# Sparse attention and experts on one core: the threshold of a score tile made by ACT, and the attention ordered anew

## The chip, the core and the metric

The kernel runs on one core of a Trainium2 chip. The core has engines that run side by side, each through its own instructions in order: PE (matrix products and transposes), DVE (vector work), ACT (a function of scale times input plus bias, element by element), POOL (GpSimd, vector work on SBUF), and SP, which here only issues DMAs. They wait for one another through semaphores. The metric is the device time of one execution in microseconds (us), lower is better, as the median of several runs.

## What is computed

Three steps follow each other: attention that keeps only the scores near the largest of their row, a layer of eight experts of which each token takes one, and a dense layer. The change is in the first.

```
q, k, v: [4, 8, 576, 64]; tau = 0.02
scores = (q @ k.T) / sqrt(64)
thresh = max(scores, -1) - tau
scores = where(scores >= thresh, scores, -1e9)
attn   = exp(scores - max(scores, -1))
attn   = attn / (sum(attn, -1) + 1e-9)
x      = (attn @ v) as [2304, 512]
... x goes to the expert with the largest cosine (8 experts, 512 -> 1024 -> 512)
... then 512 -> 2048 -> 512 with h * tanh(softplus(h))
```

## The kernel before

The 32 heads are handled in 16 pairs (`pair`). A pair's scores are nine tiles of 128 rows (`scores`, called for u from 0 to 8): four tiles of 576 columns for each head, and between them (u = 4) a wide one of 640 columns that holds the last 64 rows of both. Every product is made with operands split into a high and a low part, so most things come twice.

A score tile goes through five steps:

- PE makes the scores in a PSUM tile `D` (L544, or L540 and L541 for u = 4). A ring of four such tiles serves scores, transposes and PV products together.
- DVE takes the negative maximum of each row, `m` (L548).
- DVE makes the threshold `thr = -m - tau` (L549), one element per partition. `self.ntau` holds -tau.
- ACT makes `E = exp(scores + m)` (L550).
- DVE makes `P = (scores >= thr) * E` with the row sums (L551); `PL` for u = 4. The sums are read out by a second short instruction, DVE_READ_ACCUMULATOR, under the same line.

Behind that, PE transposes `P` (L569, and `PL` in L592), ACT and DVE or POOL split the transposed tile into `hi` and `lo` (ACT L573, L577, L578 and L597; DVE L574 and L598; POOL L579), PE multiplies with `V` (L614, L615), ACT copies the result `osb` out of PSUM (L618, L619), PE turns it back (L628), and DVE scales it into `xs` (L632).

A pair's queries and keys come by two loads, `raw` on the SP queue (L477) and `QK` on the POOL queue (L478), into two buffers each. POOL subtracts them (L485, L489), and ACT scales the queries by 1/8 in one instruction (L491). Only then can the pair's first scores start.

After every fourth pair a batch of eight heads is complete. Its rows `xs` are written to DRAM from the SP queue (L714), and a chain of small DVE instructions chooses the experts (`router`, L667 and on). After the third batch an early list of tokens is made for one expert (`early`, L756 to L793), so that the loads of that expert's weights (L1025) can be issued before the attention ends.

The order of the instructions on each engine is not the order of the code. A planner (`Plan.order`) keeps a list of operations with an assumed duration and a priority, and gives each engine at each step the operation that can start first by its own clock; among equals, the one with the lowest priority number. The table `PR` holds the numbers that are added to the tile's index to make these priorities (`S`, `max`, `thr`, `exp`, `stt` for the five steps above). The chip then runs each engine's list as planned, whatever the real durations are.

Of the kernel before, what the change touches and what calls it, by code (L numbers as in the profile page):

```python
# [12 lines left out]
AF = mybir.ActivationFunctionType  # L13
ALU = mybir.AluOpType
# [4 lines left out]
B, H, S, D = 4, 8, 576, 64  # L19
# [13 lines left out]
DF = 1024  # L33
FF = 2048
YW = DM + 2
PR = {'er': -2619.9, 'ep': 21.8, 'S': -1982.0, 'max': -153.5, 'nb': -889.1, 'exp': -5879.6, 'stt': -152.4, 'T': 7.7, 'Tp': 1782.0, 'p32': 220.7, 'hi': 779.9, 'lo': -419.6, 'dlo': -3008.1, 'pv0': 15.6, 'pv1': 20.3, 'po': 1302.8, 'osb': 1044.0, 'x': -0.4, 'px': 1519.1, 'xev': 285.6, 'q': -2270.7, 'scale': -1169.5, 'thr': -538.6, 'kl': -64.4, 'v': 3680.0, 'load': -688.7, 'dve_lo': (1, 4, 7), 'TL': 8.5, 'TLp': 1148.1, 'TLh': 593.3, 'TLl': -956.3, 'route': 1062.7, 'rkpos': 7.0, 'kl_dve': 0, 'q_pool': 2, 'of': 31.7, 'rd': -735.6, 'A_pool': (), 'nA': 0, 'n0': 2, 'ne': 375.2, 'ns': 340.5, 'nr': 2, 'np': -247.6}
PR2 = {'pipe': (), 'dve_hi': (0, 5, 6), 'xo': 28.3, 'ps': (9.4, 19.4), 'cd': 1400000.0, 'split': (("ACT", "DVE"), ("ACT", "POOL"), ("ACT", "DVE"), ("ACT", "DVE"), ("ACT", "DVE"), ("ACT", "POOL"), ("ACT", "DVE"), ("ACT", "DVE")), 'sl': 28000, 'll': 2000, 'pool_lo': (0, 2, 5, 7), 'gbuf': 4, 'lag': 792.0, 'fw': 807.0, 'fw_act': (1, 3), 'fw_pool': (1, 2, 3), 'n0': 0, 'n1': 0.85, 'np': 425.2, 'ld': -417.9, 'w0': -43.3, 'w1': -231.3, 'wlo': 312.9, 'xg': -217.3, 'xt': -648.5, 'xh': -515.6, 'h': -564.9, 'hs': -795.5, 'ht': -410.1, 'hh': -461.8, 'yy': -44.9, 'ye': 19.4, 'yi': 872.9, 'fy': 331.1, 'ft': 295.4, 'fx': 270.0, 'f1': -825.7, 'sg': -67.6, 'rc': 536.7, 'gg': 80.4, 'gh': -47.7, 'gl': -79.7, 'ob': -955.1, 'pt': -803.4}


# [3 lines left out]
def t_mm(m, n):  # L43
    return max(110, n / 2.4 + 14)


def t_act(n, psum=True, ptr=0):
    return (n + (61 if psum else 112)) / 1.2 + 93 * ptr


def t_dve(n, fast=False):
    return ((n / 2 if fast else n) + 65) / 0.96


def t_pool(n):
    return 2.25 * n + 100
# [26 lines left out]
class Plan:  # L83
# [8 lines left out]
    def add(self, eng, dur, fn, r=(), w=(), prio=0.0, lat=0, after=(), dma=0):  # L92
        i = len(self.ops)
        deps = set(after)
        for k in r:
            if k in self.last_w:
                deps.add(self.last_w[k])
            self.readers.setdefault(k, []).append(i)
        for k in w:
            if k in self.last_w:  # L100
                deps.add(self.last_w[k])
            deps.update(x for x in self.readers.get(k, ()) if x != i)
            self.last_w[k] = i
            self.readers[k] = []
        deps.discard(i)
        hs = []
        for k in list(r) + list(w):
            h = k[0] if isinstance(k, tuple) else k
            if isinstance(h, Handle) and h not in hs:
                hs.append(h)  # L110
                self.users.setdefault(h.group, []).append(i)
                if h.after is not None:
                    deps.add(h.after)
        self.ops.append([eng, dur, fn, deps, hs, prio, lat, dma, self.phase])
        return i
# [125 lines left out]
class Kernel:  # L241
# [34 lines left out]
    def h(self, pool, tag, shape, dt, bufs, at):  # L276
        key = (pool, tag)
        if key not in self.rings:
            self.rings[key] = Ring(bufs)
        return Handle(self.rings[key], lambda: self.pools[pool][0].tile(shape, dt, tag=tag, name=tag, bufs=bufs), at, pool, self.hooks.get(pool))  # L280
# [178 lines left out]
    def pair(self, p):  # L459
# [7 lines left out]
        qk, v = self.io["qk"][p], self.io["v"][p]  # L467
        pr = t0 + PR["load"]
        if p == 0:
# [10 lines left out]
        for j in range(2):  # L480
            pj = t0 + 4.5 * j
            first = p == 0 and j == 0
            on_dve = j < PR["kl_dve"]
            qe, qd = (nc.gpsimd, t_pool(S)) if j < PR["q_pool"] and not first else (nc.vector, t_dve(S))
            x = add("POOL" if qe is nc.gpsimd else "DVE", qd, lambda j=j, qe=qe: qe.tensor_tensor(QK()[64:128, j, 0:S], raw()[64:128, j], QK()[64:128, j, 0:S].bitcast(F32), op=ALU.subtract), r=[(raw, j)], w=[(QK, 1 + j)], prio=pj + PR["q"])  # L485
            if first:
                self.behind = [x]
            ke = nc.vector if on_dve else nc.gpsimd
            add("DVE" if on_dve else "POOL", t_dve(S) + 300 if on_dve else t_pool(S), lambda j=j, ke=ke: ke.tensor_tensor(KL()[:, j], raw()[:, 2 + j], QK()[:, 2 + j, 0:S].bitcast(F32), op=ALU.subtract), r=[(raw, j), (QK, 4 + j)], w=[(KL, j)], prio=pj + PR["kl"])  # L489

        add("ACT", t_act(2 * S, False), lambda: nc.scalar.mul(QK()[:, 0:2, 0:S], QK()[:, 0:2, 0:S].bitcast(F32), 0.125), w=[(QK, 1), (QK, 2)], prio=t0 + PR["scale"])  # L491
        add("SP", 600, lambda: nc.sync.dma_start(vraw(), v), w=[vraw], prio=pr + 9, lat=2000, dma=328e3, after=self.behind)
# [23 lines left out]
    def scores(self, p, u, QK, KL, Ps, PL, den, dk, denL):  # L516
        nc, add, h = self.nc, self.pl.add, self.h
        at = 9 * p + u
        sc = self.two(at)
        m = h("a_late", "m", [128, 1], F32, 6, at)  # L520
        thr = h("a_late", "thr", [128, 1], F32, 6, at)
        E = h("a_early", "E", [128, 640], F32, 3, at)
        if u == 4:
            js, i = (0, 1), None
            cols, w_ = (512, 576), 320
            outs, w = (lambda: PL()[:, :], lambda: denL()[:, 0:1]), [PL, denL]
        else:
            j, i = (0, u) if u < 4 else (1, u - 5)
            js = (j,)
            cols, w_ = (i * 128 + j * (QW + 64),), HD  # L530
            outs, w = (lambda: Ps[i]()[:, j * S:(j + 1) * S], lambda: den[:, j, i:i + 1]), [(Ps[i], j), (dk[j], i)]

        def mm():
            Qf = QK().rearrange("p a b -> p (a b)")
            for n in range(2):
                if u == 4:

                    for a, (k, jj, k0, o0) in enumerate(((320, 0, 0, 0), (256, 1, 0, 64)) if n == 0 else ((320, 1, 256, 0), (256, 0, 320, 0))):
                        for b, K in enumerate((QK()[:, 2 + jj, k0:k0 + k], KL()[:, jj, k0:k0 + k])):
                            nc.tensor.matmul(sc()[:, n, o0:o0 + k], lhsT=Qf[:, cols[jj]:cols[jj] + 128], rhs=K, start=(a == 0 and b == 0), stop=False)  # L540
                    nc.tensor.matmul(sc()[:, n, 256 * n:256 * n + 64], lhsT=self.corner[:, 64 * n:64 * n + 128], rhs=self.never, start=False, stop=True)  # L541
                    continue
                for a, K in enumerate((QK()[:, 2 + j, n * HD:(n + 1) * HD], KL()[:, j, n * HD:(n + 1) * HD])):
                    nc.tensor.matmul(sc()[:, n, :HD], lhsT=Qf[:, cols[0]:cols[0] + 128], rhs=K, start=(a == 0), stop=(a == 1))  # L544

        sv, Ev = (lambda: sc()[:, :, :w_]), (lambda: E()[:, 0:2 * w_].rearrange("p (a b) -> p a b", a=2))
        add("PE", 4 * t_mm(128, HD) if u != 4 else 4 * t_mm(128, 320) + 4 * t_mm(128, 256) + 220, mm, r=[(QK, x + j) for x in (1, 4) for j in js] + ([(QK, 3)] if u == 4 else []) + [(KL, j) for j in js], w=[sc], prio=at + PR["S"])
        add("DVE", t_dve(2 * w_), lambda: nc.vector.tensor_reduce(m(), sv(), axis=AX.XY, op=ALU.max, negate=True), r=[sc], w=[m], prio=at + PR["max"])  # L548
        add("DVE", 131, lambda: nc.vector.tensor_scalar(thr(), m(), -1.0, self.ntau, op0=ALU.mult, op1=ALU.add), r=[m], w=[thr], prio=at + PR["thr"])  # L549
        add("ACT", t_act(2 * w_, ptr=1), lambda: nc.scalar.activation(Ev(), sv(), AF.Exp, bias=m(), scale=1.0), r=[sc, m], w=[E], prio=at + PR["exp"])  # L550
        add("DVE", t_dve(2 * w_) + 65, lambda: nc.vector.scalar_tensor_tensor(outs[0]().rearrange("p (a b) -> p a b", a=2), sv(), thr(), Ev(), op0=ALU.is_ge, op1=ALU.mult, accum_out=outs[1]()), r=[sc, thr, E], w=w, prio=at + PR["stt"])  # L551

# [907 lines left out]
```

## Time and profile before

| | |
|---|---|
| median of 3 runs | 1101.08 us (1101.04 to 1101.51) |
| the profiled execution | 1099.78 us, its span 1098.0 us |
| attention, first to last score tile | 14 to 365 us of the span |
| its drain, and the choice of experts | 365 to 402 us |
| experts, then the dense layer | 402 us to the end |

The profile is of one execution. The span is the time from its first to its last instruction; the execution's own time is 1.8 us longer. "Busy" is time in which an engine runs an instruction. Instructions of one engine overlap a little, so a step from the start of one to the start of the next tells more of what it costs than its duration. What ends an idle stretch is called its releaser.

### The profile page before, as it was taken

The numbers are of one execution on the slowest core, as the hardware profiler recorded it, in microseconds if no ns is written. First come the engines' busy times: TensorE is split into PE (matmuls) and PEld (weight loads), VectorE is DVE, ScalarE is ACT, GpSimd is POOL, SyncE is SP. The second block draws the span as 40 slices with busy tenths as digits, with TensorE's granted clock in tenths as the row PEclk, the third lists the DMA queues.
The fourth block names the chain that finished last, engine by engine and source line by source line (L and its number), as shares of the span: only waits on it lengthen the run. The fifth ranks groups of instructions, "written<-read, shape, count | busy, mean of one in ns | idle before, by whom it ended". The sixth has DMA issues, their size and how long they took to land. (4 is left out here: it accounts for less than half of the span.)

```text
span 1098.0 us, 17382 instructions
## 1 busy us (share of the span) xinstructions
PE 1003.5 (91%) x6397; PEld 911.0 (83%) x6397; DVE 838.6 (76%) x1318; ACT 625.3 (57%) x1077; POOL 519.6 (47%) x495
## 2 busy tenths in 40 slices
PE   3899879979989969999999986999999999999997
PEld 3788778868888858979999975899999899998986
DVE  6899879978999676846678794997867768677580
ACT  4688768867877635534555543555445354453540
POOL 7688667857866523323342263633322333323322
PEclk9899899998999969999999997999999999999999
DMA  9844965694593299967679866000010100100001
GB/s 293 247 123 125 140 165 155 139 126 122 180 110 63 101 105 350 320 218 267 252 264 330 319 208 214 21 20 20 20 40 10 30 21 20 39 11 10 21 1 38
DMA packets 84700, 144.32 MB, mean 131 GB/s; under 512 B 47936, under 2 KB 47936, under 8 KB 78592
## 3 DMA queue, kind: packets, MB, share of 16 engines
q1 hardware_dynamic: 51392, 105.23, 34.6%
q0 software_dynamic: 33216, 37.93, 13.6%
q8 instruction: 51, 0.84, 0.3%
q14 instruction: 41, 0.34, 0.1%
HBM read 116.07 MB, written 27.06 MB: 130 GB/s over the span
## 5 line engine op out<-in xcount | busy, mean ns | idle before, releaser
L1322 DVE RECIPROCAL b<-p 128x512 f32<-128x512 f32 x72 | 239.3, 3339 | 19.7 <-ACT p L1319 18.2
L1325 POOL TENSOR_TENSOR lo<-c,hi 128x512 fp32r<-128x512 f32 x72 | 93.4, 1304 | 138.8 <-ACT hi L1324 127.5
L579 POOL TENSOR_TENSOR lo<-p,hi 128x512 fp32r<-128x512 f32 x96 | 122.7, 1286 | 59.4 <-ACT hi L578 51.7
L548 DVE TENSOR_REDUCE m<-D 128x1 f32<-128x576 f32 x144 | 107.5, 755 | 19.7 <-PE D L544 18.5
L550 ACT ACTIVATE E<-D,m 128x576 f32<-128x576 f32 x144 | 104.6, 751 | 21.5 <-DVE m L548 20.9
L1317 ACT ACTIVATE p<-S 128x512 f32<-128x512 f32 x72 | 43.0, 597 | 125.3 <-PE S L1304 115.3
L544 PE MATMUL D<-QK 128*128 128x288 f32 x256 | 85.3, 348 | 22.6 <-ACT QK L491 11.3
L551 DVE SCALAR_TENSOR_TENSOR P<-D,thr,E 128x576 f32<-128x576 f32 x128 | 101.9, 810 | 0.7 <-ACT E L550 0.4
L1323 DVE SCALAR_TENSOR_TENSOR c<-b,S 128x512 f32<-128x512 f32 x72 | 46.1, 656 | 71.6 <-POOL lo L1325 71.6
L569 PE MATMUL D<-ident,P 128*128 128x128 f32 x576 | 84.0, 283 | 13.1 <-DVE P L551 10.9
L991 DVE TENSOR_TENSOR wl<-raw,wh 128x1024 fp32r<-128x1024 f32 x48 | 63.3, 1339 | 36.3 <-ACT wh L989 29.7
L1082 PE MATMUL S<-xh,wh 128*128 128x256 f32 (+1 forms) x288 | 88.6, 307 | 0.0
L1082 PE MATMUL S<-xh,wl 128*128 128x256 f32 (+1 forms) x288 | 87.9, 305 | 0.1
L1082 PE MATMUL S<-xl,wh 128*128 128x256 f32 (+1 forms) x288 | 87.7, 304 | 0.0
L1304 PE MATMUL S<-hi,wh 128*128 128x256 f32 x288 | 82.3, 286 | 2.3 <-DVE c L1323 2.2
L614 PE MATMUL D<-hi,V 128*128 128x512 f32 x160 | 74.1, 463 | 10.3 <-DVE PL L551 9.4
L1304 PE MATMUL S<-lo,wh 128*128 128x256 f32 x288 | 82.2, 285 | 0.0
L1304 PE MATMUL S<-hi,wl 128*128 128x256 f32 x288 | 82.1, 285 | 0.0
L1324 ACT CAST hi<-c 128x512 fp32r<-128x512 f32 x72 | 43.9, 618 | 65.9 <-PE B L1332 52.1
L569 PEld LDWEIGHTS D<-ident,P 128*128 128x128 f32 x576 | 66.6, 148 | 16.6 <-issue 11.7
L991 POOL TENSOR_TENSOR wl<-raw,wh 128x1024 fp32r<-128x1024 f32 x16 | 40.1, 2505 | 79.4 <-ACT wh L989 79.4
L544 PEld LDWEIGHTS D<-QK 128*128 128x128 f32 x256 | 52.0, 203 | 28.6 <-ACT QK L491 11.3
(262 smaller groups left out, 3172.0 us busy)
## 6 DMA issues: line engine op xcount, KB each, us to landing
raw<-in_wm_dram SPq DMA_DIRECT2D x32, 1024.0 KB, 7.5
raw<-in_qk_dram SPq DMA_DIRECT2D x15, 1152.0 KB, 5.2
QK<-in_qk_dram POOLq DMA_DIRECT2D x15, 1152.0 KB, 8.6
fraw<-in_w_in_dram SPq DMA_DIRECT2D x16, 512.0 KB, 5.9
fraw<-in_w_out_dram SPq DMA_DIRECT2D x16, 512.0 KB, 6.7
y_dram<-osb SPq DMA_DIRECT2D x21, 257.0 KB, 5.3
vraw<-in_v_dram SPq DMA_DIRECT2D x16, 320.0 KB, 5.8
V<-in_v_dram POOLq DMA_DIRECT2D x16, 320.0 KB, 4.0
```

Source lines behind the costliest of these rows:

```text
L544: nc.tensor.matmul(sc()[:, n, :HD], lhsT=Qf[:, cols[0]:cols[0] + 128], rhs=K, start=(a == 0), stop=(a == 1))
L548: add("DVE", t_dve(2 * w_), lambda: nc.vector.tensor_reduce(m(), sv(), axis=AX.XY, op=ALU.max, negate=True), r=[sc], w=[m], prio=at + PR[" ...
L550: add("ACT", t_act(2 * w_, ptr=1), lambda: nc.scalar.activation(Ev(), sv(), AF.Exp, bias=m(), scale=1.0), r=[sc, m], w=[E], prio=at + PR[" ...
L551: add("DVE", t_dve(2 * w_) + 65, lambda: nc.vector.scalar_tensor_tensor(outs[0]().rearrange("p (a b) -> p a b", a=2), sv(), thr(), Ev(), o ...
L569: pd(nc.tensor.transpose(pt()[:, i * 128:(i + 1) * 128], Ps[i]()[:, c * 128:(c + 1) * 128], self.ident))
L579: add("POOL", t_pool(512), lambda: nc.gpsimd.tensor_tensor(lo(), p32(), hi().bitcast(F32), op=ALU.subtract), r=[p32, hi], w=[lo], prio=at ...
L614: nc.tensor.matmul(o(), lhsT=w, rhs=T[c][b](), start=(a == 0 and b == 0), stop=(a == 4 and b == 1))
L991: add(le, d, lambda: e.tensor_tensor(lo()[:, s], raw()[:, s], hi()[:, s].bitcast(F32), op=ALU.subtract), r=[kr, kh], w=[kl], prio=prio + .5)
L1082: hd(nc.tensor.matmul(hp().rearrange("p (k n) -> p k n", n=128), lhsT=a()[:, kc, f], rhs=x()[:, k0:k0 + n, kc * 128:(kc + 1) * 128], start ...
L1304: hd(nc.tensor.matmul(hp()[:, f * 256:(f + 1) * 256], lhsT=w, rhs=x, start=(n == 0), stop=(n == 11)))
L1322: add("DVE", 3270, lambda q_=q_, r_=r_: v.reciprocal(r_(), g2(q_)), r=[q_], w=[r_], prio=au + R["rc"])
L1325: add("POOL", t_pool(512), lambda gg=gg, gh=gh, gl=gl: g.tensor_tensor(g2(gl), gg(), g2(gh).bitcast(F32), op=ALU.subtract), r=[gg, gh], w= ...
```

## The change

The threshold moves from DVE to ACT: the same value, made by an activation with the identity function, scale -1 and the bias `ntau`, instead of a multiply and an add. The planner is told of 130 ns on ACT instead of 131 on DVE. And most numbers of the table `PR` are set anew, so that the planner orders the whole attention differently on all engines. `PR2`, which orders the experts and the dense layer, is as it was, and behind the dispatch every engine's order is unchanged.

```
-PR = {..., 'S': -1982.0, 'max': -153.5, 'exp': -5879.6, 'stt': -152.4, ..., 'thr': -538.6, ..., 'load': -688.7, 'TL': 8.5, ...}
+PR = {..., 'S': -2172.6, 'max': -56.7, 'exp': -3405.4, 'stt': -0.3, ..., 'thr': -14.3, ..., 'load': -124.9, 'TL': 13.9, ...}
...
-        add("DVE", 131, lambda: nc.vector.tensor_scalar(thr(), m(), -1.0, self.ntau, op0=ALU.mult, op1=ALU.add), r=[m], w=[thr], prio=at + PR["thr"])
+        add("ACT", 130, lambda: nc.scalar.activation(thr(), m(), AF.Identity, scale=-1.0, bias=self.ntau), r=[m], w=[thr], prio=at + PR["thr"])
```

What this does to the order is seen at two places. The first is DVE in the middle of the attention, behind the row sums' reciprocal of one pair. `m` is a maximum, `thr` a threshold, `P` and `PL` the products with `E`, `lo` a low part, `xs` the scaled output. Before:

```order
L548 TENSOR_REDUCE m<-D 128x1 x2
L549 TENSOR_SCALAR thr<-m,ntau 128x1 x2
L548 TENSOR_REDUCE m<-D 128x1
L551 SCALAR_TENSOR_TENSOR P,den_85<-D,thr,E 128x576
L549 TENSOR_SCALAR thr<-m,ntau 128x1
L551 SCALAR_TENSOR_TENSOR P,den_85<-D,thr,E 128x576 x2
L574 TENSOR_TENSOR lo<-D,hi 128x512
L548 TENSOR_REDUCE m<-D 128x1
L549 TENSOR_SCALAR thr<-m,ntau 128x1
L548 TENSOR_REDUCE m<-D 128x1
L551 SCALAR_TENSOR_TENSOR P,den_85<-D,thr,E 128x576
```

And in the changed kernel, from the same place:

```order
L548 TENSOR_REDUCE m<-D 128x1 x2
L551 SCALAR_TENSOR_TENSOR P,den_85<-D,thr,E 128x576 x2
L548 TENSOR_REDUCE m<-D 128x1
L574 TENSOR_TENSOR lo<-D,hi 128x512
L548 TENSOR_REDUCE m<-D 128x1
L551 SCALAR_TENSOR_TENSOR P,den_85<-D,thr,E 128x576
L632 TENSOR_TENSOR xs<-D,rd 128x5x72
L551 SCALAR_TENSOR_TENSOR PL,denL<-D,thr,E 128x640
```

The thresholds are gone, and what stood between a maximum and its product has become less: here one product, or a subtraction and a maximum.

The second is ACT while the second batch is being written to DRAM. `E` is an exponential (128x640 is the wide tile u = 4), `p` and `hi` are parts of a transposed tile, `TL` that of the wide tile, `rt` the router's. L491 is the scaling that waits for the next pair's load. Before:

```order
L726 ACTIVATE rt<-rt 128x40
L577 COPY p_4412<-D 128x512
L550 ACTIVATE E<-D,m 128x576
L578 CAST hi<-p_4412 128x512
L491 ACTIVATE QK<-QK 128x2x576
L550 ACTIVATE E<-D,m 128x640
L577 COPY p_4482<-D 128x512
L578 CAST hi<-p_4482 128x512
```

And in the changed kernel, around the same L491:

```order
L550 ACTIVATE E<-D,m 128x576
L549 ACTIVATE thr<-m,ntau 128x1
L597 CAST TL<-D 128x10x64
L550 ACTIVATE E<-D,m 128x640
L491 ACTIVATE QK<-QK 128x2x576
L549 ACTIVATE thr<-m,ntau 128x1
L577 COPY p_4472<-D 128x512
L578 CAST hi<-p_4472 128x512
```

The wide tile's exponential has moved ahead of L491, and its threshold stands behind it.

## Rows read from the trace of the kernel before

**Rows 1.** The page: the span, and the busy time of every engine with its instructions.

```profile
span 1098.0 us, 17382 instructions
...
PE 1003.5 (91%) x6397; PEld 911.0 (83%) x6397; DVE 838.6 (76%) x1318; ACT 625.3 (57%) x1077; POOL 519.6 (47%) x495
```

**Rows 2.** Windows: us, then busy us (instructions) of PE, PEld, DVE, ACT, POOL; PEclk, DMA share, GB/s.

```profile
14.00:365.00 351.00, 307.29 (x2097) 280.05 (x2097) 315.82 (x773) 270.80 (x490) 255.96 (x235) 0.95 0.69 146
...
122.00:150.00 28.00, 23.77 (x157) 21.92 (x156) 25.58 (x66) 19.66 (x41) 14.07 (x13) 0.88 1.14 139
...
216.00:243.00 27.00, 22.66 (x152) 20.29 (x151) 24.96 (x65) 19.26 (x40) 13.63 (x12) 0.94 1.15 144
...
311.00:336.00 25.00, 20.79 (x138) 18.79 (x136) 23.18 (x59) 17.62 (x38) 14.55 (x13) 0.93 1.12 109
```

**Rows 3.** Windows of 23 us, columns as above; the last row is L548 alone (DVE).

```profile
83.00:106.00 23.00, 22.02 (x156) 20.10 (x155) 21.45 (x55) 20.02 (x36) 19.69 (x18) 1.00 0.47 132
...
336.00:359.00 23.00, 21.07 (x153) 19.05 (x153) 22.38 (x53) 19.66 (x35) 17.50 (x15) 1.00 0.30 44
...
83.00:106.00 23.00, 8.12 (x11) 1.00 0.47 132
```

**Rows 4.** Timeline of DVE: start us, us, engine, instruction, count, idle time before and releaser.

```profile
209.07 0.76 DVE L548 TENSOR_REDUCE m<-D 128x1 f32<-128x576 f32 x1
209.74 0.81 DVE L551 SCALAR_TENSOR_TENSOR P<-D,thr,E 128x576 f32<-128x576 f32 x1
...
210.48 0.21 DVE L549 TENSOR_SCALAR thr<-m,ntau 128x1 f32<-128x1 f32 x1
210.60 0.81 DVE L551 SCALAR_TENSOR_TENSOR P<-D,thr,E 128x576 f32<-128x576 f32 x1
...
212.50 0.69 DVE L574 TENSOR_TENSOR lo<-D,hi 128x512 fp32r<-128x512 f32 x1 [0.34 <-ACT hi L573]
213.10 0.75 DVE L548 TENSOR_REDUCE m<-D 128x1 f32<-128x576 f32 x1
213.89 0.21 DVE L549 TENSOR_SCALAR thr<-m,ntau 128x1 f32<-128x1 f32 x1
214.02 0.81 DVE L548 TENSOR_REDUCE m<-D 128x1 f32<-128x640 f32 x1
```

**Rows 5.** Timeline of ACT, the same microseconds and columns.

```profile
208.78 2.00 ACT L550 ACTIVATE E<-D,m 128x576 f32<-128x576 f32 x3
...
211.80 0.59 ACT L573 CAST hi<-D 128x512 fp32r<-128x512 f32 x1
212.28 0.61 ACT L577 COPY p<-D 128x512 f32<-128x512 f32 x1
212.75 0.30 ACT L619 COPY osb<-D 128x128 f32<-128x128 f32 x1
212.92 0.65 ACT L578 CAST hi<-p 128x512 fp32r<-128x512 f32 x1
213.88 0.74 ACT L550 ACTIVATE E<-D,m 128x576 f32<-128x576 f32 x1 [0.32 <-DVE m L548]
```

**Rows 6.** Timeline of SP, POOL, ACT and DVE around the first batch that is complete.

```profile
122.56 1.00 SPq L714 DMA_DIRECT2D x_dram<-xs  x2
...
149.96 2.77 POOL L485 TENSOR_TENSOR QK<-raw,QK 64x576 fp32r<-64x576 f32 x2 [6.32 <-issue]
...
152.76 1.16 ACT L491 ACTIVATE QK<-QK 128x1152 fp32r<-128x1152 f32 x1 [4.80 <-POOL QK L485]
...
154.64 0.88 DVE L551 SCALAR_TENSOR_TENSOR PL<-D,thr,E 128x640 f32<-128x640 f32 x1 [4.77 <-ACT E L550]
```

**Rows 7.** Timeline of SP and PE behind the last score tile.

```profile
373.58 1.11 SPq L1025 DMA_DIRECT2D raw<-in_wm_dram  x2
...
376.50 0.52 PE L786 MATMUL D<-M,A 128*128 128x4 bf16 x15 [2.18 <-DVE M L779]
```

More of the change, by code (lines that the diff above doesn't have):

```diff
@@ L35 @@
 YW = DM + 2
-PR = {'er': -2619.9, 'ep': 21.8, 'S': -1982.0, 'max': -153.5, 'nb': -889.1, 'exp': -5879.6, 'stt': -152.4, 'T': 7.7, 'Tp': 1782.0, 'p32': 220.7, 'hi': 779.9, 'lo': -419.6, 'dlo': -3008.1, 'pv0': 15.6, 'pv1': 20.3, 'po': 1302.8, 'osb': 1044.0, 'x': -0.4, 'px': 1519.1, 'xev': 285.6, 'q': -2270.7, 'scale': -1169.5, 'thr': -538.6, 'kl': -64.4, 'v': 3680.0, 'load': -688.7, 'dve_lo': (1, 4, 7), 'TL': 8.5, 'TLp': 1148.1, 'TLh': 593.3, 'TLl': -956.3, 'route': 1062.7, 'rkpos': 7.0, 'kl_dve': 0, 'q_pool': 2, 'of': 31.7, 'rd': -735.6, 'A_pool': (), 'nA': 0, 'n0': 2, 'ne': 375.2, 'ns': 340.5, 'nr': 2, 'np': -247.6}
+PR = {'er': -3405.1, 'ep': 17.4, 'S': -2172.6, 'max': -56.7, 'nb': -889.1, 'exp': -3405.4, 'stt': -0.3, 'T': 7.9, 'Tp': 1979.4, 'p32': 1109.3, 'hi': 1626.2, 'lo': -141.9, 'dlo': -3206.2, 'pv0': 14.5, 'pv1': 20.7, 'po': 71.2, 'osb': 1407.1, 'x': -0.3, 'px': 3492.6, 'xev': 910.6, 'q': -1369.2, 'scale': -542.9, 'thr': -14.3, 'kl': -46.6, 'v': 3922.5, 'load': -124.9, 'dve_lo': (1, 4, 7), 'TL': 13.9, 'TLp': 1176.9, 'TLh': 1078.9, 'TLl': -1498.9, 'route': 2313.3, 'rkpos': 8.6, 'kl_dve': 0, 'q_pool': 2, 'of': 31.7, 'rd': -65.1, 'A_pool': (), 'nA': 0, 'n0': 2, 'ne': 375.2, 'ns': 340.5, 'nr': 2, 'np': -247.6}
 PR2 = {'pipe': (), 'dve_hi': (0, 5, 6), 'xo': 28.3, 'ps': (9.4, 19.4), 'cd': 1400000.0, 'split': (("ACT", "DVE"), ("ACT", "POOL"), ("ACT", "DVE"), ("ACT", "DVE"), ("ACT", "DVE"), ("ACT", "POOL"), ("ACT", "DVE"), ("ACT", "DVE")), 'sl': 28000, 'll': 2000, 'pool_lo': (0, 2, 5, 7), 'gbuf': 4, 'lag': 792.0, 'fw': 807.0, 'fw_act': (1, 3), 'fw_pool': (1, 2, 3), 'n0': 0, 'n1': 0.85, 'np': 425.2, 'ld': -417.9, 'w0': -43.3, 'w1': -231.3, 'wlo': 312.9, 'xg': -217.3, 'xt': -648.5, 'xh': -515.6, 'h': -564.9, 'hs': -795.5, 'ht': -410.1, 'hh': -461.8, 'yy': -44.9, 'ye': 19.4, 'yi': 872.9, 'fy': 331.1, 'ft': 295.4, 'fx': 270.0, 'f1': -825.7, 'sg': -67.6, 'rc': 536.7, 'gg': 80.4, 'gh': -47.7, 'gl': -79.7, 'ob': -955.1, 'pt': -803.4}
```

## The prediction, made before the changed kernel had run

> **What bounds the kernel now.** I read the page first [rows 1]: a span of 1098.0 us, DVE busy for 76% of it and ACT for 57%. Those shares mix four stages, so they say little. The diff changes the attention's score tiles and the numbers that order the attention; on every engine the order behind the dispatch is the same in both kernels. So I read the attention alone, from its first score tile to its last (14 to 365 us), with the view of windows [rows 2]: DVE is busy for 315.8 of these 351 us (90%), PE for 307.3, ACT for 270.8.
>
> Then I looked for what is not compute. Each time a batch of heads is complete, its rows are written to DRAM from the SP queue, and the loads of the pair after next come behind them. The timeline around the first of these [rows 6] shows the writes from 122.6 us, GpSimd idle for 6.3 us until the next QK has landed (149.96), ACT idle for 4.8 us at the scaling of that QK, L491, and DVE idle for 4.8 us, because the exponential that it waits for is queued on ACT behind L491. Three stretches of 28, 27 and 25 us have a DMA share above 1.1 [rows 2]. They end with a transfer; faster compute buys nothing in them. That leaves 351 - 80 = 271 us in which compute sets the pace.
>
> In an undisturbed stretch of those, 83 to 106 us [rows 3], DVE is busy for 21.45 of 23 us (93.3%), ACT for 20.02 (87%), and 11 tile maxima start. At 336 to 359 us DVE reaches 22.38 (97.3%): the highest share that I saw one of these two hold in such a window. So DVE sets the pace there, and ACT is only 1.4 us a window behind it. That is the number to keep in mind.
>
> **What leaves DVE.** 144 instructions of L549. Each lasts 0.21 us, but instructions overlap, so I take steps from start to start [rows 4]. A maximum followed by something independent is one step of 0.67 us (209.07 to 209.74). Followed by its own threshold it takes 0.79 (213.10 to 213.89) and the threshold another 0.13, so 0.25 us are saved. A threshold that stands elsewhere costs 0.12 (210.48 to 210.60). In the order before, 40 of the 144 stand right behind their own maximum and 104 don't: 40 x 0.25 + 104 x 0.12 = 22.5 us, 0.156 a tile. If all of it passed through in the stretches bound by compute, it would be 22.5 x 271 / 351 = 17.4 us. In the window of 23 us DVE would fall to 21.45 - 11 x 0.156 = 19.7 us.
>
> **What comes to ACT.** 144 activations of one element with a bias from memory; no row shows that form. Bounds from steps on ACT [rows 5]: the copy L619 of 128 elements takes a step of 0.17 us (212.75 to 212.92), a cast of 512 one of 0.48 (211.80 to 212.28), so 0.0008 us an element and about 0.07 for one element without the pointer. Three exponentials take 2.00 us, so a step of (2.00 - 0.74) / 2 = 0.63; less 575 x 0.0008 that leaves 0.17. The exponential too has a pointer for its bias, so it is the nearest row, and I take 0.17: 24.5 us in all, with 0.07 as the low end and 0.26 (a whole duration of such an instruction, nothing overlapped: 0.74 - 0.48) as the high one. In the window ACT goes to 20.02 + 11 x 0.17 = 21.9 us of 23: **ACT becomes the busiest engine**, and the window cannot go below that.
>
> The Trainium skill, page "ScalarE: Activation LUTs", section "What ACT_TABLE_LOAD costs", gives such an activation with a pointer about 280 ns plus 0.833 ns an element, with about 93 ns of overlap; an estimate from that page is 0.19 us a step and 27 us in all, which would make ACT's window 22.1 us. No run here shows it yet.
>
> **The new wait.** The last DVE step of a tile (L551) now needs two results of ACT. By the rows: a maximum ends at 213.85, its exponential starts at 213.88 [rows 5] and the threshold would start 0.63 us behind it, last 0.26 and be seen by DVE about 0.11 us later (the gap from the cast that ends at 212.39 to L574 at 212.50 [rows 4]): 214.88, where the exponential alone would be seen at 214.73. So each tile's chain is 0.15 us longer. One instruction in between keeps DVE busy until about 0.6 us behind the maximum, against 1.03 needed: a wait of about 0.4 us. In the changed order 33 of 144 tiles have just one instruction in between, the others two or more, so at most about 14 us of waits. They fit into the room that DVE gains (2.8 us in each of some 12 windows: 33 us), so I don't add them; they are why DVE won't set the pace any more, and if the cover is gone they cost up to 14 us.
>
> The order shows something else: at two of the three DMA stretches a threshold stands on ACT right **behind L491**, the instruction that waits for the late QK. At the second, the exponential of the wide tile moves ahead of L491, which would free it from that wait, but its threshold stays behind. So L551 of that tile waits as long as now, about 4.8 us [rows 6], and the PV products with it. The stalls stay; I count neither gain nor loss.
>
> **What is moved.** TL's transposes come five score tiles later, and V's products begin a tile earlier or later; the same instructions on the same engines, nothing added, and for PE there is cover in the 351 - 307.3 us of idle time. The loads keep their places on POOL to within one instruction of 1.3 us, and SP keeps the pattern of writes, then loads. After the last score tile the drain has another mix of transposes and products, with the same wait for the early list; what that wait is worth is 2.2 us [rows 7], so up to 2 us either way, and I take zero. The first loads of the experts' weights are issued at 373.6 us [rows 7], right behind the early choice of an expert, so they come as much earlier as the attention does: I expect what the attention gains to pass through to the end.
>
> **The sum.** ACT, at 21.9 us of work in the window and the 97.3% that DVE reaches, makes the window 22.5 us: 0.5 us of 23, 2.2%, of 271 us 5.9. No gain in 80 us, none in the drain. The profiled execution took 1099.8 us (span 1098.0), 1.3 under the median of 1101.1, so 1093.8 in such a profile, and **1095 us** as a median.
>
> **Rivals.**
> 1. DVE's whole saving arrives: ACT's step is nearer to 0.07 (window work 20.8 us), and DVE's waits fall between its own instructions. For it: ACT is idle for a quarter of the attention. Against it: the nearest row says 0.17. Up to 17.4 us: 1084.
> 2. Slower, by ACT as the new pace: everything on ACT is in order, and it also feeds POOL and the transposes, so it may not be kept as busy as DVE can be. The point that decides is a share of 95.2% (21.9 of 23). At DVE's usual 93.3% the window becomes 23.5 us: 0.5 us longer, 2.0% of 271 us, +5.5: 1107. With 0.26 a step ACT has 22.9 us to do in the window, and it is slower at any share that a row shows. For it: ACT's idle time today is mostly waiting for PE and DVE, which doesn't vanish. The Trainium skill states the same choice as a rule (page "ScalarE: Activation LUTs", section "Rules for kernel authors"): multiply and add belong on VectorE, not ScalarE. It reasons by cost per element, and no run here shows it for one element.
> 3. No change: saving and new waits cancel. The DMA stretches end when they end, and in between PE, DVE and ACT are all within 10% of each other, so each waits a little for the others: within 2.2 us of 1101.
>
> **How the numbers follow.** 0.2% of this time is 2.2 us, about what a measurement can tell from no change. Forecast (3 to 10 us less) 0.45; the whole saving (over 10 us less) 0.15; no change 0.19; slower 0.21. Faster takes the first two and a little of the third: 0.62; same 0.17; slower 0.21. The range runs from rival 1's 1084 to 1106, just short of rival 2's price. The forecast's own range is 1091 to 1098.
>
> **What would show it.** Right: L549 on ACT with a step near 0.17 us and 144 of them; ACT's busy share in an undisturbed 23 us above 93% and DVE's near 86%; the maxima 2% closer together; L491 still waiting 4 to 5 us at three places, with L551 behind it. Wrong: DVE still above 93% and the attention 15 us shorter (rival 1), or L551 waiting for L549 at far more than 33 tiles with ACT below 95% (rival 2). I would be most wrong if the moved transposes and products let PE run denser, or tear gaps that the order doesn't show: the granted clock is below full in the stalls (0.88 at 122 to 150 us [rows 2]), and more of them would cost PE twice.

## The result and the profile after

The changed kernel took 1118.1 us as the median of four executions, before 1101.3 us beside it on the same chip. One of the four (2965.84 us) is left out of the ratio; the others are 1115.14, 1115.88 and 1120.32, so that the middle one is 1115.88, 14.6 us above before. The profile is of the 1120.32. The ratio is **1.0125, 95% interval 1.009 to 1.0161**: slower by 1.25%, outside the predicted range, on the side to which I had given 0.21.

The page of the changed kernel, with the lines that answer to [rows 1]:

```profile
span 1118.3 us, 17273 instructions
...
PE 1009.2 (90%) x6397; PEld 914.5 (82%) x6397; DVE 826.9 (74%) x1174; ACT 649.2 (58%) x1221; POOL 521.8 (47%) x495
```

144 instructions have gone from DVE to ACT: DVE is busy for 11.7 us less, ACT for 23.9 more. Yet PE's busy time, for which no instruction was added, rose by 5.7 us. The windows answer to [rows 2, 3]: the attention to the end of its last score tile, the same 23 us as before, and the maxima (L548) in them. Columns as in [rows 2]: length, then busy us of PE, PEld, DVE, ACT, POOL.

```profile
14.00:379.30 365.30, 312.29 (x2094) 282.31 (x2093) 305.58 (x629) 293.98 (x631) 255.86 (x237) 0.94 0.67 141
83.00:106.00 23.00, 21.29 (x150) 18.84 (x148) 19.15 (x42) 20.97 (x43) 19.04 (x17) 1.00 0.41 123
...
83.00:106.00 23.00, 7.56 (x10) 1.00 0.41 123
```

The attention ends at 379.3 us; before it ended at 364.6. DVE is down to 83% of the undisturbed window (the prediction had about 86), ACT is at 91% (above 93), and in the same 23 us ten maxima start, not eleven. Neither engine is at a limit there, and the kernel is slower.

The view of one line, for the new activation: durations in ns (least, median, most), and who waited for it, in us and times.

```profile
L549 ACT ACTIVATE thr<-m,ntau x144: 279/293/342, 14.4 to 380.9; 128x1 f32<-128x1 f32 x144
...
  DVE P L551: 13.8, 31
  DVE PL L551: 6.8, 4
```

L551 waits for the threshold 31 + 4 times, 20.6 us in all. I first took that for the cause. The runs below show that it isn't.

**Where the time went.** Two timelines show one of the places. First ACT, around 172 us:

```profile
171.10 0.58 ACT L577 COPY p<-D 128x512 f32<-128x512 f32 x1 [0.53 <-PE D L569]
171.58 0.75 ACT L550 ACTIVATE E<-D,m 128x576 f32<-128x576 f32 x1
172.21 0.29 ACT L549 ACTIVATE thr<-m,ntau 128x1 f32<-128x1 f32 x1
172.40 0.58 ACT L577 COPY p<-D 128x512 f32<-128x512 f32 x1
```

Then PE at the same time:

```profile
169.88 0.30 PE L544 MATMUL D<-QK 128*128 128x288 f32 x1
170.01 0.29 PE L544 MATMUL D<-KL,QK 128*128 128x288 f32 x1
170.35 1.09 PE L569 MATMUL D<-ident,P 128*128 128x128 f32 x8
173.04 0.40 PE L544 MATMUL D<-QK 128*128 128x288 f32 x1 [1.59 <-ACT p L577]
...
173.91 0.44 PE L544 MATMUL D<-QK 128*128 128x288 f32 x1
174.15 0.44 PE L544 MATMUL D<-KL,QK 128*128 128x288 f32 x1
...
174.87 0.63 PE L614 MATMUL D<-hi,V 128*128 128x512 f32 x1
...
176.85 0.45 PE L614 MATMUL D<-hi,V 128*128 128x512 f32 x1
```

And the window behind the wait (PEclk is the column after the five engines):

```profile
173.00:177.00 4.00, 3.96 (x15) 3.58 (x16) 2.19 (x6) 1.92 (x5) 2.00 (x2) 0.57 0.25 83
```

PE transposes two blocks at 170.35 into one slot of D, whose ring has four. The next score tile needs a free slot, and the one that comes free is the transposed one, once both copies L577 have read it. The second copy stands on ACT behind an exponential and its threshold: it runs from 172.40 to 172.98, and PE starts at 173.04, after 1.59 us idle. That is not all. Before the wait a score matmul came every 0.13 us (169.88, 170.01); behind it they come every 0.24 (173.91, 174.15), and the granted clock from 173 to 177 is 0.57 of full, a mixture of 2.4 and 1.2 GHz. How much this pair lost is seen on DVE, from one product of a wide tile to the next, in the changed kernel and then before:

```profile
160.09 0.88 DVE L551 SCALAR_TENSOR_TENSOR PL<-D,thr,E 128x640 f32<-128x640 f32 x1
...
184.13 0.89 DVE L551 SCALAR_TENSOR_TENSOR PL<-D,thr,E 128x640 f32<-128x640 f32 x1 [0.27 <-ACT thr L549]
```

```profile
154.64 0.88 DVE L551 SCALAR_TENSOR_TENSOR PL<-D,thr,E 128x640 f32<-128x640 f32 x1 [4.77 <-ACT E L550]
...
176.11 0.87 DVE L551 SCALAR_TENSOR_TENSOR PL<-D,thr,E 128x640 f32<-128x640 f32 x1
```

That is 24.0 us for 21.5. The rest of the loss is spread: the fourth pair's PL comes 4.0 us later than before, the eighth's 8.0, the last one's 14.2.

Over the attention the view of waits has 45 waits of PE with 52.5 us in the changed kernel, 43 with 43.5 us before, and PE's busy time is 312.3 us for 306.9. These are the 14.7 us: 9.0 more of waiting, 5.4 more for the same matmuls. Of the 5.4 the clock explains about 2: by the granted clock in the trace PE is busy at 1.2 GHz for 35.0 us of the attention, before for 31.0, and what takes twice as long there loses half of the difference (an estimate). The rest comes at full clock, and no run shows why.

Nor is the wait shown above the kind that grew: for L577's copies PE (L544) waits 5.6 us in all, before 7.3. New are six waits for the low part of TL (L598), 10.8 us. The two long ones stand where the first batch is written to DRAM:

```profile
131.81 0.33 PE L615 MATMUL D<-TL,V 128*128 128x128 f32 x1 [4.59 <-DVE TL L598]
...
159.57 0.79 PE L614 MATMUL D<-hi,V 128*128 128x512 f32 x1 [5.25 <-DVE TL L598]
```

On DVE the first of these low parts stands behind the small instructions that choose the experts (L667 to L672):

```profile
129.93 1.09 DVE L672 SCALAR_TENSOR_TENSOR oh<-rt 128x40 f32<-128x40 f32 x1
130.94 0.81 DVE L598 TENSOR_TENSOR TL<-D,TL 128x640 fp32r<-128x640 f32 x1
```

The second waits for TL's first copy (L597), which stands on ACT behind L491 and so behind the late QK. Before, PE waited 3.67 and 4.75 us in that stretch, for P behind the same small instructions and for PL behind L491. So both places cost PE a wait in either kernel; in the changed one it comes by way of TL, whose move the prediction had put at no cost, and is 1.4 us longer in all.

### The profile page after: what moved, and what is told of

The parts are those of the page before. It is cut to its first block, busy times and chain, and to the rows that moved or that the text cites. A ratio compares the mean times of both kernels' runs of the same rounds, so it can differ in the third digit from the quotient of the medians.

```text
span 1118.3 us, 17273 instructions
## 1 busy us (share of the span) xinstructions
PE 1009.2 (90%) x6397; PEld 914.5 (82%) x6397; DVE 826.9 (74%) x1174; ACT 649.2 (58%) x1221; POOL 521.8 (47%) x495
## 5 line engine op out<-in xcount | busy, mean ns | idle before, releaser
L548 DVE TENSOR_REDUCE m<-D 128x1 f32<-128x576 f32 x144 | 107.1, 755 | 29.8 <-PE D L544 27.0
L550 ACT ACTIVATE E<-D,m 128x576 f32<-128x576 f32 x144 | 106.9, 754 | 31.0 <-DVE m L548 30.0
L544 PE MATMUL D<-QK 128*128 128x288 f32 x256 | 87.3, 355 | 31.8 <-ACT QK L491 11.6
L551 DVE SCALAR_TENSOR_TENSOR P<-D,thr,E 128x576 f32<-128x576 f32 x128 | 102.4, 812 | 14.4 <-ACT thr L549 13.8
L569 PE MATMUL D<-ident,P 128*128 128x128 f32 x576 | 87.3, 290 | 13.6 <-DVE P L551 5.4
L1323 DVE SCALAR_TENSOR_TENSOR c<-b,S 128x512 f32<-128x512 f32 x72 | 46.1, 656 | 71.6 <-POOL lo L1325 71.6
L991 DVE TENSOR_TENSOR wl<-raw,wh 128x1024 fp32r<-128x1024 f32 x48 | 61.6, 1303 | 38.6 <-ACT wh L989 30.9
L569 PEld LDWEIGHTS D<-ident,P 128*128 128x128 f32 x576 | 69.3, 149 | 18.9 <-issue 11.8
L544 PEld LDWEIGHTS D<-QK 128*128 128x128 f32 x256 | 52.4, 205 | 37.9 <-ACT QK L491 11.6
```

Source lines behind the costliest of these rows:

```text
L569: pd(nc.tensor.transpose(pt()[:, i * 128:(i + 1) * 128], Ps[i]()[:, c * 128:(c + 1) * 128], self.ident))
L991: add(le, d, lambda: e.tensor_tensor(lo()[:, s], raw()[:, s], hi()[:, s].bitcast(F32), op=ALU.subtract), r=[kr, kh], w=[kl], prio=prio + .5)
```

## Experiments

Two theories were set against each other at first: A, the engine (thresholds on ACT make ACT, or L551's wait for them, the pace), and B, the order (the new sequence on every engine makes PE wait). A program that emits on one engine what the planner placed on another separates them. The ratio is always to the kernel before on the same chip, and "attention" is the stretch from 14 us to the end of the last score tile of the profiled execution (before: 350.6 us).

**e4_old_lists_act: before's order on every engine; only the threshold is issued on ACT.**

```diff
-add("DVE", 131, lambda: nc.vector.tensor_scalar(thr(), m(), -1.0, self.ntau, ...
+add("DVE", 131, lambda: nc.scalar.activation(thr(), m(), AF.Identity, scale=-1.0, bias=self.ntau), ...
```

> The order of before on every engine, with only the 144 thresholds issued on ACT at their planned places. Theory A (the engine: a threshold on ACT lengthens each tile's chain, and L551 waits for it): slower than before by most of the 14 us, 1108 to 1116. Theory B (the new order of the attention costs it): within 4 us of before, 1097 to 1105, with L551 waiting for L549 under 8 us in all.

Measured: 1100.77 us, 0.9971 [0.9942, 1.0]. The windows of the attention and of two undisturbed pairs, and behind them those of before:

```profile
14.00:362.90 348.90, 310.61 (x2094) 281.19 (x2094) 299.07 (x629) 296.17 (x631) 255.83 (x238) 0.95 0.70 147
71.80:111.60 39.80, 38.68 (x275) 34.89 (x274) 35.01 (x73) 37.25 (x79) 33.24 (x28) 1.00 0.54 153
```

```profile
73.30:113.20 39.90, 37.92 (x274) 34.84 (x274) 36.93 (x92) 34.02 (x61) 33.27 (x28) 1.00 0.54 154
14.00:364.60 350.60, 306.89 (x2094) 279.65 (x2093) 315.42 (x772) 270.40 (x489) 255.56 (x235) 0.95 0.69 146
```

Two pairs last 39.8 us for 39.9, though DVE has 1.9 us less to do and ACT 3.2 more. One part of the expectation missed: L551's wait for the threshold is not under 8 us but nearly what it is in the changed kernel, and the attention is no longer for it. From the view of L551, us and times:

```profile
  ACT thr L549: 17.5, 19
```

**e5_old_lists_act_again** is the same kernel, measured more often.

> The same kernel as e4_old_lists_act (before's order on every engine, the threshold merely issued on ACT), in more rounds, since 0.9971 with an interval up to 1.0 leaves open whether the move gains anything. If PE sets the pace, the move gives only what shorter waits of PE give (37.5 us for 43.5 in its profile): 0.996 to 1.0. If DVE's relief counts, 0.98 to 0.99.

Measured: 1103.91 us, 1.0008 [0.9982, 1.0034]; attention 351.2 us. Together with e4 the move by itself makes no difference that these runs can tell. The profiles of e4 and e5, of one and the same kernel, have attentions of 348.9 and 351.2 us: a difference of 2 to 3 us between two profiles says nothing.

**e3_new_lists_dve: the changed kernel's order on every engine; the threshold is issued on DVE.**

```diff
-add("ACT", 130, lambda: nc.scalar.activation(thr(), m(), AF.Identity, ...
+add("ACT", 130, lambda: nc.vector.tensor_scalar(thr(), m(), -1.0, self.ntau, ...
```

> The changed order on every engine, with only the thresholds issued on DVE at their planned places. Theory A: back to 1098 to 1104. Theory B: stays slow, 1111 to 1120, with DVE's waits for score tiles above 18 us and L551's wait for ACT gone.

Measured: 1122.7 us, 1.0153 [1.0109, 1.0197]. Its attention, and PE's wait at the place shown above:

```profile
14.00:386.40 372.40, 318.84 (x2094) 287.64 (x2093) 322.50 (x772) 271.85 (x489) 256.72 (x237) 0.92 0.66 138
...
174.90 0.40 PE L544 MATMUL D<-QK 128*128 128x288 f32 x1 [1.41 <-ACT p L577]
175.13 0.29 PE L544 MATMUL D<-KL,QK 128*128 128x288 f32 x1
175.26 0.29 PE L544 MATMUL D<-QK 128*128 128x288 f32 x1
```

With no threshold on ACT the wait for the slot is still there, 1.41 us, 0.18 shorter: about the step of a threshold on ACT (0.19, from 172.21 to 172.40). Behind it the matmuls come every 0.13 us: here the wait was not followed by a slower clock, as it was in the changed kernel. L551's wait for ACT is down to 1.3 us, and the kernel is as slow. With e4 and e5 this makes four cases, two orders by two engines, and only the order matters: A has fallen, B holds, and the loss comes with the order.

**e1_engine_only** keeps the old table of priorities and gives the planner the threshold on ACT; **e2_table_only** takes the new table and leaves the threshold on DVE.

```diff
 e1, against before:
-add("DVE", 131, lambda: nc.vector.tensor_scalar(thr(), ...
+add("ACT", 130, lambda: nc.scalar.activation(thr(), ...
 e2, against before:
-PR = {'er': -2619.9, 'ep': 21.8, ...
+PR = {'er': -3405.1, 'ep': 17.4, ...
```

> The old table of priorities, the threshold planned and issued on ACT, so that the planner orders anew by the old numbers. Theory A: slower than before by 8 us or more. Theory B: this order is new as well, so anything from 1095 to 1112; if under 1101, the move itself can gain and the table took it away.

> The new table, the threshold planned and issued on DVE. Theory A: within 5 us of before. Theory B: slow, 1108 to 1120, as the table is made for another load of the engines.

Measured: e1 1133.58 us, 1.0272 [1.023, 1.0313]; e2 1104.99 us, 1.0012 [0.9989, 1.0034]. Both are outside what B had foreseen and within what A had, so by themselves they would have misled. But in both the planner made another order, as e3 and e4 did not, so they don't test the engine. The new table alone costs nothing; the old table with the engine changed in the plan costs more than the whole change. Priorities are read by a planner that takes, on each engine, what it thinks is ready first, so a changed engine makes it choose anew everywhere. e1's attention, and two undisturbed pairs:

```profile
14.00:388.60 374.60, 315.62 (x2096) 280.85 (x2094) 296.47 (x630) 296.20 (x631) 255.24 (x238) 0.95 0.66 137
77.70:121.00 43.30, 38.64 (x275) 34.91 (x274) 34.84 (x73) 37.24 (x79) 33.16 (x28) 1.00 0.50 140
```

The clock is full, PE has the same 38.6 us of work as in e4, and the two pairs take 43.3 us. What is added are short waits of PE, none over 1.1 us there; in the whole attention it has 72 waits with 58.8 us.

**f4_old_table_150: before, with only the planner's number for DVE's threshold at 150 in place of 131.** Every instruction and its engine stay.

```diff
-add("DVE", 131, lambda: nc.vector.tensor_scalar(thr(), ...
+add("DVE", 150, lambda: nc.vector.tensor_scalar(thr(), ...
```

> The kernel before in every operation and engine; only the planner's number for the threshold on DVE is 150 in place of 131, so the planner sets another order from the same table. If what costs in the changed kernel is that a new plan leaves an order in which PE, the pace, waited little, this shows it without a threshold on ACT and without new priorities: slower than before, ratio 1.003 to 1.015, with PE's waits in the attention above before's 43.5 us. If the order matters only through the new priorities or through ACT's queue, it is within 0.2% of before.

Measured: 1117.67 us, **1.0142 [1.0115, 1.017]**. One number that runs nowhere on the chip costs as much as the whole change. Its windows (the attention, two undisturbed pairs, 6 us of a later stretch), and a row of PE's timeline ahead of these 6 us:

```profile
14.00:384.00 370.00, 322.12 (x2095) 294.96 (x2093) 311.46 (x772) 270.90 (x489) 255.20 (x237) 0.90 0.67 139
75.50:115.40 39.90, 37.93 (x274) 34.88 (x274) 36.93 (x92) 34.02 (x61) 33.26 (x28) 1.00 0.54 154
...
258.00:261.00 3.00, 3.00 (x14) 3.00 (x14) 2.55 (x7) 1.57 (x3) 2.98 (x3) 0.50 0.43 114
261.00:264.00 3.00, 3.00 (x11) 2.61 (x11) 1.73 (x5) 0.00 (x0) 0.00 (x0) 0.50 0.94 385
...
254.52 1.94 PE L569 MATMUL D<-ident,P 128*128 128x128 f32 x8 [3.66 <-DVE lo L574]
```

The undisturbed pairs are those of before to a few hundredths. Most of the loss lies in the stretches in which a batch is written to DRAM, as at this place: PE waits 3.66 us, runs at a granted clock of 0.50 (1.2 GHz) behind the wait, and is busy for 100% of 258 to 264 us at half speed, while DVE falls to 1.73 of 3 us and ACT to nothing. In the attention PE waits 4 us longer than before and is busy 15 us longer, for the same matmuls. Here the clock explains it: PE is busy at 1.2 GHz for 61.2 us, before for 31.0, and half of the difference is the 15.

**h1_hi_back: the changed kernel with one priority set back.**

```diff
-'hi': 1626.2
+'hi': 779.9
```

> The changed kernel with one number of its table set back, that of the second copy of a transposed tile on ACT (L578, hi, from 1626.2 to the old 779.9), so that these copies stand earlier among ACT's operations. If the 14.7 us that the attention lost lie in single places of the order where PE waits for a copy or for what is made from it (two waits of L614 for lo, 4.3 and 2.9 us, and those that follow), part of it comes back: attention 356 to 362 us for 365.3, ratio 1.003 to 1.01. If the loss lies in ACT's load with the threshold, no order of the copies helps: ratio 1.01 to 1.016.

Measured: 1110.33 us, 1.0083 [1.0056, 1.0109].

```profile
14.00:372.60 358.60, 311.82 (x2094) 283.30 (x2094) 304.52 (x629) 294.31 (x631) 255.39 (x238) 0.94 0.68 143
```

The attention is 358.6 us: 6.7 of the 14.7 us come back, with ACT's load as it was. That isn't the worth of these copies' place alone: the planner set another order on every engine, so this too is one more order of the same work.

**h2_new_search: a third table, planned with 190 ns for the threshold on ACT.**

```diff
-PR = {'er': -3405.1, 'ep': 17.4, ... 'hi': 1626.2, ... 'thr': -14.3, ...
+PR = {'er': -3574.8, 'ep': 18.8, ... 'hi': 779.9, ... 'thr': -684.0, ...
...
-add("ACT", 130, lambda: nc.scalar.activation(thr(), ...
+add("ACT", 190, lambda: nc.scalar.activation(thr(), ...
```

> The threshold on ACT as in the changed kernel, planned at 190 ns for the 0.19 us that the trace of after shows, with a third table of priorities (er, ep, S, stt, Tp, hi, px, xev, thr and rkpos differ from the new one). If the engine is not what costs, a new plan with the threshold on ACT can come near before, though nothing on PE gets shorter: ratio 0.998 to 1.01. If the engine costs, 1.01 to 1.03, as both tables gave with a plan that had the threshold on ACT (1.0125 and 1.0272).

Measured: 1110.63 us, 1.0087 [1.0061, 1.0113]; attention 358.7 us. Better than the changed kernel, not as good as before. All four plans with the threshold on ACT (the changed kernel, e1, h1, h2) are slower than before; of the two new plans with it on DVE one is (f4), one isn't (e2).

The order explains the loss, but not why the relief of DVE gave nothing in the old order. The last four runs ask which engine sets the pace there.

**f1_no_threshold: before's order, no threshold on any engine.** L551 compares with the constant -tau, so it selects other elements, and the experts get other rows; the whole time (1423.54 us) says nothing, the attention does.

```diff
-add("DVE", 131, lambda: nc.vector.tensor_scalar(thr(), m(), ...
+add("DVE", 131, lambda: None, ...
-... sv(), thr(), Ev(), op0=ALU.is_ge, ...
+... sv(), self.ntau, Ev(), op0=ALU.is_ge, ...
```

> Before's order, with the 144 threshold operations left out altogether: L551 compares each score with the constant -tau, so other elements pass and the routing behind the attention differs; only the attention (from 14 us to the end of the last score tile, 350.6 us in before) is compared. If DVE sets the pace, as the prediction had it, the attention loses most of the 22.5 us that the thresholds take on DVE: 328 to 335 us. If PE sets the pace (PE busy 306.9 us plus its own 43.5 us of waits make up the 350.6), an operation that is gone from DVE and put on no other engine gives no more than the run with the threshold on ACT in the same order, which had 348.9: 345 to 350 us.

Measured, in the windows of the attention and of two undisturbed pairs:

```profile
14.00:366.10 352.10, 306.10 (x2094) 280.72 (x2093) 297.23 (x629) 270.85 (x489) 255.60 (x237) 0.94 0.70 145
71.20:111.00 39.80, 37.76 (x274) 34.82 (x274) 34.66 (x74) 34.05 (x61) 33.22 (x28) 1.00 0.55 155
```

352.1 us, 1.5 more than before (a little above what either expectation had), and two pairs in 39.8 us, with DVE at 34.7 us of work and ACT at 34.1. DVE has 2.3 us less to do in two pairs, and nothing comes of it. So what DVE was freed of could not be gained in this order, wherever it went.

**f2_less_pe_dve: before's order, without the matmuls of the keys' low parts (320 of PE's); f3_less_pe_act: the same, with the threshold issued on ACT.** The scores lack that part; the wide tile loses it by the same edit in its own loop.

```diff
-for a, K in enumerate((QK()[:, 2 + j, ...], KL()[:, j, ...])):
+for a, K in enumerate((QK()[:, 2 + j, ...],)):
```

> Before's order and engines, with the matmuls of the keys' low parts (KL) left out of every score tile on PE: 320 matmuls fewer, about 50 us of PE's busy time by their share of its rows; nothing on DVE or ACT changes. If DVE sets the pace (315.8 us busy of 351), the attention stays within 3 us of 350.6. If PE sets it, the attention gets shorter until DVE's 316 us and its waits stop it: 328 to 340 us, the whole 10 to 22 us faster (ratio 0.98 to 0.99).

> As f2_less_pe_dve, with the threshold issued on ACT, in the same order. If PE was the pace and DVE is the next one behind it, the move that was worth 1.7 us of the attention with PE's full work is worth 8 to 17 us of it now, since DVE's work falls from about 316 to 294 us: attention 315 to 328 us, ratio 0.97 to 0.98. If the move is worth nothing whatever PE does (ACT's queue or the wait for the threshold takes it back), it is within 3 us of f2_less_pe_dve.

Measured: f2 1094.62 us, 0.9931 [0.9902, 0.996]; f3 1101.36 us, 0.9973 [0.9951, 0.9995]. f2, then f3:

```profile
14.00:353.30 339.30, 286.23 (x1774) 244.43 (x1775) 312.40 (x769) 269.47 (x487) 254.25 (x234) 0.94 0.72 151
69.70:107.80 38.10, 35.19 (x234) 29.84 (x234) 36.63 (x91) 34.01 (x61) 33.03 (x28) 1.00 0.58 164
```

```profile
14.00:363.40 349.40, 287.71 (x1775) 245.39 (x1775) 298.37 (x629) 292.38 (x631) 255.32 (x238) 0.93 0.70 147
71.30:110.60 39.30, 35.19 (x234) 29.74 (x234) 35.22 (x73) 36.81 (x79) 33.18 (x28) 1.00 0.56 158
```

Less work on PE shortens two pairs from 39.9 to 38.1 us, where fewer operations on DVE had shortened nothing: PE was the pace. It had 37.9 of 39.9 us (95%). One rival is left: with fewer matmuls each score tile is also ready earlier, and no run tells PE's work from this shorter way of a tile through the engines. In f2 DVE has 36.6 of 38.1 (96%) and by its share is the next limit, 1.8 us below. The attention, 11.3 us shorter, is at the edge of what I expected, the ratio above it; 20.7 us of PE's busy time went, not 50. f3 goes against its expectation: with DVE now the limit, the move to ACT should have gained, and two pairs take 39.3 us. ACT is now the busiest, 36.8 us of 39.3 (94%), with PE and DVE at 90%. That is what rival 2 described, but it is argued from the shares alone: e4 has ACT at the same 94% and costs nothing.

**g1_e_domain: before's order, no threshold; L551 compares E with exp(-tau) (`etau`, made once), so it reads E twice and no PSUM.** It was to free D's slots earlier.

```diff
-... sv(), thr(), Ev(), op0=ALU.is_ge, op1=ALU.mult, ...
+... Ev(), self.etau, Ev(), op0=ALU.is_ge, op1=ALU.mult, ...
```

> Before's order, no threshold operation: the selection compares the exponential E with exp(-tau), made once at the start, in place of comparing the score with the maximum less tau, so it selects the same elements up to rounding. L551 then reads no PSUM, and a score tile's slot of D comes free with the exponential, 1 to 3 us earlier. If PE sets the pace and some of its 43.5 us of waits are for slots held until L551 (DVE P ends 10.9 us of them at L569, which is data and stays, and a few us at L544), the attention gains 2 to 8 us: ratio 0.993 to 0.998. If DVE sets the pace, L551 no longer waits for thr and 22.5 us are gone: ratio 0.98 to 0.986.

Measured: 1150.61 us, **1.0431 [1.0412, 1.045]**, outside both. The rows: two pairs, L551's durations in ns, and two of its instructions on DVE; then GpSimd at the same times.

```profile
83.30:132.10 48.80, 39.64 (x277) 36.45 (x276) 46.10 (x74) 34.35 (x61) 37.11 (x28) 0.97 0.44 125
...
L551 DVE SCALAR_TENSOR_TENSOR P<-E,etau x128: 802/1108/3623, 14.7 to 415.5; 128x576 f32<-128x576 f32 x128
...
87.35 0.81 DVE L551 SCALAR_TENSOR_TENSOR P<-E,etau 128x576 f32<-128x576 f32 x1
...
95.30 1.58 DVE L551 SCALAR_TENSOR_TENSOR P<-E,etau 128x576 f32<-128x576 f32 x1
```

```profile
87.42 1.00 POOL L493 DMA_DIRECT2D V<-in_v_dram  x1 [1.36 <-PE D L615]
...
94.98 1.28 POOL L579 TENSOR_TENSOR lo<-p,hi 128x512 fp32r<-128x512 f32 x1
```

L551 takes a median of 1108 ns, at most 3623; before it took 810 on average. While GpSimd issues a DMA (87.42) it takes 0.81 us, while GpSimd subtracts (94.98 and on) 1.58. GpSimd's own subtractions suffer too: L489 has a median of 1932 ns for 1425 before. With DVE made longer so, it is the pace: 46.1 us of 48.8 (94%). The Trainium skill says of this (page "SBUF — State Buffer", section "SBUF: two separate sides") that a VectorE operation with two SBUF inputs takes an exclusive port pair against a GpSimd operation that reads SBUF, and the other blocks; the trace agrees in who is slow and when.

## Why the prediction was wrong, step by step

- **"So DVE sets the pace there": this step failed.** I had 93.3% for DVE beside 22.02 of 23 us for PE in the very same row [rows 3], and never weighed the 95.7%. f1 took the thresholds away altogether and gained nothing; f2 took work from PE and gained. A gain on DVE had no way to the end, so even with the old order there was nothing to forecast: 0.9971 and, in more executions, 1.0008 [0.9982, 1.0034], for the 0.9945 of my 1095 us.
- **"for PE there is cover in the 351 - 307.3 us of idle time": the same error, and the costlier one.** The transposes, products and copies that moved I costed at zero. The idle time of the engine that sets the pace is no cover: it is waits already paid, and a new one adds to them. The order cost 14.7 us of the attention with the threshold on ACT, and no less with it on DVE (1.0125 and 1.0153); for TL, which it moved, PE now waits 10.8 us and before not at all, though part of this stands in for other waits. The last sentence of the prediction named this ("tear gaps that the order doesn't show", and the clock that makes PE pay twice), as what would make me most wrong, but gave it no price and no chance.
- **What leaves DVE, 22.5 us:** too large. In before's order DVE's busy time in the attention fell from 315.4 to 299.1 us (e4) or 297.2 (f1): 16 to 18 us.
- **What comes to ACT, 0.17 us a step, 24.5 us:** right, a little low. The step is 0.19 (172.21 to 172.40), the duration 293 ns, and ACT's busy time rose by 25.8 us in before's order (e4). The estimate from the Trainium skill's page "ScalarE: Activation LUTs", section "What ACT_TABLE_LOAD costs", 280 ns and 0.19 us, agrees better with the step than my row.
- **The new wait, at most 14 us:** 13.8 us in 31 tiles of 576 columns, for 33 foreseen, and 6.8 more in four wide tiles. Of these, 4.60 us (257.69) are the stall behind L491 that the prediction kept apart; the other three, 1.2 us at most, add to the new wait. In e3 these waits don't exist, and it is as slow: covered, as I said.
- **The stalls at L491 stay:** right for two of the three places: it waits 6.65 us at 156.91 and 4.30 at 256.31 for GpSimd's L485 (before 4.80 and 4.64). At the third, where before waited 2.35 us, it doesn't.
- **"They end with a transfer; faster compute buys nothing in them":** only in part. Each of the three stretches of before also holds a wait of PE for P, behind the small instructions that choose the experts on DVE, which no transfer ends. From the view of PE's waits before:

```profile
PE D L569 <- DVE P L551: 10.9, 3, 3.7
```

- **Passes through to the end:** right. The attention lost 14.7 us, and the dispatch (L864) starts at 415.65 for 401.79, 13.9 later. The drain between, 36.4 us for 37.2, was rightly put at zero within 2. The profiled execution loses some 6 us more behind the dispatch; its span is 1118.3, those of the two other executions 1113.4 and 1113.9, and every engine's order is the same there, so that is left out.
- **Rival 2 (ACT as the pace)** gave the right sign for a reason that didn't hold here, so the 0.21 on slower was luck: e4 and e5 have ACT at 37.2 of 39.8 us and cost nothing. A loss by the move itself appears only once PE is relieved (f3 beside f2). The Trainium skill's rule that multiply and add belong on VectorE (the same page, "Rules for kernel authors") agrees with that run, and not with the kernel as it is, where e5 shows no difference.

What stays open: which of the new order's places cost how much. The pair with the wait shown above lost 2.6; the rest is spread over waits that no run took away one by one, and h1, which gives back 6.7 us, is another order throughout. Why PE's busy time rises at full clock (e4: 3.7 us more than before, at the same 0.95) is open too. No version here that computes the same beats before beyond what the runs can tell.

## What to carry to other kernels

Ask of each engine, in the same undisturbed window, how near it is to full, even if the diff doesn't touch it. Where several are above 85%, as here, the shares don't decide: take some work off each in turn, with the order kept (f1, f2), and see which one shortens the window. Where a busy time rises with no instruction added, look at the clock, which explains it in f4 and only in part in the changed kernel. When a list scheduler sets the order, a change of one cost or one engine is a change of the whole order, and its price must be taken as that of an unknown reordering, in this kernel 0 to 2.7%, a loss in five of the six new orders. To test a move by itself, keep the old order and change only the engine that issues it.

## What the runs showed of the hardware that I had not expected

- A wait of PE can be paid again behind it. After 3.66 us of waiting (f4, 254.52) PE ran at 1.2 GHz through at least 264 us, 100% busy from 258; after 1.59 us (until 173.04 in the changed kernel) it ran at a mixture of both clocks until about 177. After 1.41 us at the same place of e3 it ran on at full speed.
- The selection on DVE (L551), 128x576, took 0.81 us with one of its two tensors in PSUM, and 1.11 us (median) with both in SBUF beside a busy GpSimd, whose subtraction of the same shape went from 1.43 to 1.93 us.
- An activation of one element with a pointer bias takes 0.29 us on ACT and 0.19 from start to start; the DVE operation that it replaces 0.21.
